# A three-stage attention and expert kernel: the conversion of one weight matrix is moved from each expert's first layer into its second

## The chip, the cores and the metric

The kernel runs on one core of a Trainium2 chip. The metric is the device time of one launch, in microseconds (us). The core has five engines that run their own instruction streams in order: TensorE (PE in the profile, with its weight loads as PEld), VectorE (DVE), ScalarE (ACT), GpSimd (POOL) and SyncE (SP, here only a queue that starts transfers). They wait for each other and for transfers through semaphores.

## The reference, cut to what matters

```python
def reference(**kwargs):
    attn_out = _attn_ref(**attn_kwargs)          # attention, the 32 largest scores of each row
    x = ...reshape(B * S, H * D)                 # 2304 rows of 512
    x = _moe_ref(x=x, **moe_kwargs)
    return _moe2_ref(x=x, **moe2_kwargs)

def _moe_ref(x, w_skip, w_gate, w1, w2):         # 8 experts, one per row, rows may skip
    ...
    for e in range(E):
        mask = e_idx == e
        h = np.maximum(xc[mask] @ w1[e], 0.0)    # 512 -> 1024, the expert's first layer
        y[mask] = gate_w[mask, None] * (h @ w2[e])  # 1024 -> 512, its second layer
    out[do_compute] = xc + y

def _moe2_ref(x, w_in, w_out):                   # every row
    h = x @ w_in                                 # 512 -> 2048, the up-projection
    g = h * (1.0 / (1.0 + np.exp(-1.702 * h)))
    return (g @ w_out).astype(np.float32)
```

`w_in` and `w_out` come as 64-bit floats; the other arrays are 32-bit.

## The kernel before, in words

The program has three stages, one after the other: attention with the choice of experts (up to about 507 us of the profiled span), the eight experts (to about 697 us), and the up- and down-projection over all 2304 rows (to the end).

**The experts.** They are done in eight turns of a Python loop, in an order that puts the four experts with most rows on the even turns. An even turn (from here on a long turn) has room for 192 rows, an odd one (a short turn) for 128. What each turn does on each engine follows from the order in which the loop writes the instructions; nothing reorders them.

- `layer1` runs 8 steps f, one for each 128 columns of `w1`. A step is 4 matmuls, which the trace shows as 8 records, so 64 in a turn; `ph` is a step's result in PSUM and has four buffers. In each step ACT writes the high part of the hidden values (`hb`, line 928), DVE the low part (line 930), and `step(f)` is called.
- `step(f)` calls `split_w2`: ACT makes the high part `w2h` of 128 rows of `w2` (line 967), DVE or POOL the low part `w2l` (line 968). At f = 0 POOL also gathers the rows `xg` of the next turn from DRAM, and at f = 0 and 4 it scatters finished rows `xo` to DRAM, where there are any.
- Between the layers PE transposes the gathered rows of the next turn (`turn`, lines 914 to 918: `xgT`).
- `layer2` multiplies `hb` with `w2h` and `w2l` (`py`, line 945): 40 matmuls in a long turn, of which 16 are for its second piece of 64 rows and come first, and 24 in a short one. ACT and DVE then combine the results (`yo`, lines 951 and 952, only in long turns; `xo`, lines 948 and 953).

**The conversion of w_in.** `w_in` is cut into 16 pieces of 128 x 512 numbers. `split_f64` is a Python generator with three parts. The first starts the transfer of a piece of 64-bit numbers into `raw`; the second makes 32-bit numbers `t` of it with three DVE instructions (lines 865 to 867); the third makes a high part `wih` on ACT (line 870) and a low part `wil` on POOL (line 871). A long turn converts three pieces, a short turn one. In the kernel before, the pieces of a turn are asked for at the turn's start and at f = 0 and 4, and their second and third parts are written into the steps f = 2 to 7 of that same turn's `layer1`. `raw` has two buffers. The results are used only in the third stage.

**Transfers.** SP starts the loads of `w1` (2 MB a turn, `w1t`, two buffers), of `w2` (eight loads of 256 KB, one buffer each, so the load for the next turn waits until this turn's conversion has read the buffer) and of `raw` (512 KB each), in the order in which the program writes them. POOL starts gathers and scatters.

Of the kernel before, what the change touches and what calls it, by code (L numbers as in the profile page):

```python
# [11 lines left out]
I32 = mybir.dt.int32  # L12
AF = mybir.ActivationFunctionType
ALU = mybir.AluOpType
# [15 lines left out]
def body(ctx: ExitStack, tc: tile.TileContext, q, k, v, w_skip, w_gate, w1, w2, w_in, w_out, out):  # L30
    nc = tc.nc
    V, A, G, T, SY = nc.vector, nc.scalar, nc.gpsimd, nc.tensor, nc.sync
    P = 128
    B, H, S, D = q.shape
    NT, DM = out.shape
    E, _, F = w1.shape
    DFF = w_in.shape[1]
# [53 lines left out]
    def load_w1(e):  # L91
        w1t = ew.tile([P, KC, F], F32, name="w1t")
        if isinstance(e, int):
            SY.dma_start(w1t, w1[e].rearrange("(c p) f -> p c f", p=P))
        else:
            SY.dma_start(w1t, w1[bass.ds(e, 1), :, :].rearrange("o (c p) f -> p (o c) f", p=P))
        return w1t
# [19 lines left out]
    def fetch_rows(xg, ix, src=XD):  # L117
        G.indirect_dma_start(
            out=xg, out_offset=None, in_=src, in_offset=bass.IndirectOffsetOnAxis(ap=ix, axis=0)
        )  # L120
# [6 lines left out]
    with ExitStack() as ph:  # L127
# [116 lines left out]
        def warm(k):  # L244
            for _ in range(k):
                T.matmul(Y, ones[:, :P], ones, start=True, stop=True)
# [445 lines left out]
        todo = []  # L692
# [16 lines left out]
        for n in range(NTL + 17):  # L709
# [5 lines left out]
            if n == NTL // 2:  # L715
                w1t = load_w1(0)
# [140 lines left out]
            first_rows()  # L857

    def split_f64(pool, src, hi, lo, queue=SY):
        raw = pool.tile([P, DFF // 4, 2], I32, name="raw")  # L860
        queue.dma_start(raw.rearrange("p n w -> p (n w)"), src.bitcast(I32))
        yield
        t = pool.tile([P, DFF // 4], I32, name="t")
        u = pool.tile([P, DFF // 4], I32, name="u")
        V.tensor_scalar(t, raw[:, :, 1], 3, 0x3FFFFFF8, op0=ALU.logical_shift_left, op1=ALU.bitwise_and)
        V.scalar_tensor_tensor(u, raw[:, :, 1], -0x40000000, t, op0=ALU.bitwise_and, op1=ALU.bitwise_or)
        V.scalar_tensor_tensor(t, raw[:, :, 0], 29, u, op0=ALU.logical_shift_right, op1=ALU.bitwise_or)
        yield
        wf = t.bitcast(F32)
        A.activation(hi, wf, AF.Copy)  # L870
        G.tensor_tensor(lo, wf, hi.bitcast(F32), op=ALU.subtract)
        yield

    fw = ctx.enter_context(tc.tile_pool(name="fw", bufs=1))
# [4 lines left out]
    def out_weights(pool, pf):  # L879
        f = len(woh)  # L880
        woh.append(pool.tile([P, DM], F32R, name=f"woh{f}"))
        wol.append(pool.tile([P, DM], F32R, name=f"wol{f}"))
        return split_f64(pf, w_out[f * P : (f + 1) * P, :], woh[f], wol[f])


    with ExitStack() as ph:
        ph.enter_context(tc.manual_schedule())
        wt = ph.enter_context(tc.tile_pool(name="wt", bufs=2))
# [11 lines left out]
        def gather(tiles):  # L900
            xgs = []
            for ix, rows in tiles:
                xg = ew.tile([P, DM + 1], F32, name="xg", bufs=4)
                fetch_rows(xg[:rows], ix)
                xgs.append(xg)
            return xgs

        def turn(tiles, xgs):
            xgT = mp.tile([P, KC, NS], F32, name="xgT")
            o = 0  # L910
            for (_, rows), xg in zip(tiles, xgs):
                pt = pT.tile([P, KC, P], F32, name="pt")
                for c in range(KC):
                    T.transpose(pt[:, c, :rows], xg[:rows, c * P : (c + 1) * P], ident[:rows, :rows])
                if o:
                    A.activation(xgT[:, :, o : o + rows], pt[:, :, :rows], AF.Copy)
                else:
                    V.tensor_copy(xgT[:, :, :rows], pt[:, :, :rows])
                o += rows
            return xgT  # L920

        def layer1(w1t, xgT, ns, step):
            hb = mp.tile([P, FC1, 2 * NS], F32R, name="hb", bufs=1)
            for f in range(FC1):
                ph_ = pH.tile([P, NS], F32, name="ph")
                for c in range(KC):
                    T.matmul(ph_[:, :ns], w1t[:, c, f * P : (f + 1) * P], xgT[:, c, :ns], start=(c == 0), stop=(c == KC - 1))  # L927
                A.activation(hb[:, f, :ns], ph_[:, :ns], AF.Relu)
                for a, b in ((0, 2 * P), (P, NS))[: 1 + (ns > P)]:
                    V.scalar_tensor_tensor(hb[:, f, b : b + min(P, ns - a)], ph_[:, a : min(a + P, ns)], 0.0,  # L930
                                           hb[:, f, a : min(a + P, ns)].bitcast(F32), op0=ALU.max, op1=ALU.subtract)
                step(f)
            return hb

        def layer2(hb, ws, tiles, xgs):
            for (ix, rows), xg in reversed(list(zip(tiles, xgs))):
                py = pY.tile([P, DM], F32, name="py")
                xo = mp.tile([P, DM], F32, name="xo")
                if rows < P:
                    parts = [(P, 0), (P, 1)]  # L940
                else:
                    parts = [(0, 0), (0, 1), (2 * P, 0)]
                for f in range(FC1):
                    for u, (o, b) in enumerate(parts):
                        T.matmul(py, hb[:, f, o : o + P], ws[b][f], start=(f == 0 and u == 0),  # L945
                                 stop=(f == FC1 - 1 and u == len(parts) - 1))
                if rows == P:
                    V.scalar_tensor_tensor(xo, py, xg[:, DM:], xg[:, :DM], op0=ALU.mult, op1=ALU.add)  # L948
                else:
                    yo = mp.tile([P, DM], F32, name="yo", bufs=1)  # L950
                    A.activation(yo[:rows], py[rows:, :], AF.Copy)
                    V.tensor_tensor(yo[:rows], py[:rows, :], yo[:rows], op=ALU.add)
                    V.scalar_tensor_tensor(xo[:rows], yo[:rows], xg[:rows, DM:], xg[:rows, :DM], op0=ALU.mult, op1=ALU.add)
                late.append((ix, xo[:rows]))

        def scatter():
            ix, xo = late.pop(0)
            G.indirect_dma_start(
                out=X2D, out_offset=bass.IndirectOffsetOnAxis(ap=ix, axis=0), in_=xo, in_offset=None,
            )  # L960
# [11 lines left out]
        todo = []  # L972
        for c in range(KC):
            for u in range(4):
                us = slice(u * DFF // 4, (u + 1) * DFF // 4)
                todo.append(split_f64(wt, w_in[c * P : (c + 1) * P, us], wih[:, c, us], wil[:, c, us],
                                      SY if todo[1:] else A))

        turns = [0, 4, 1, 5, 2, 6, 3, 7]
        slots = []  # L980
        for k in turns:
            slots.append([(IXS[:, k, :1], P)] + ([(IXS[: NS - P, k, 1:], NS - P)] if k < BIGS else []))
        who = [0]
        for k in turns[1:]:
            who.append(nc.values_load(flags[:, 2 + E + k : 3 + E + k], engines=[mybir.EngineType.SP], min_val=0, max_val=E - 1))
        nxt = []
        xgs = x0
        warm(10)
        nx = turn(slots[0], xgs)
        for e in range(E):  # L990
            w1n = load_w1(who[e + 1]) if e + 1 < E else None
            long = turns[e] < BIGS
            ns = NS if long else P
            convs = [todo.pop(0) for _ in range(1 if e % 2 else 3)]
            ws = ([], [])

            def step(f):
                split_w2(raws, ws, f, long)
                if f == 0:
                    for g in convs[:2]:  # L1000
                        next(g)
                    if e + 1 < E:
                        nxt.append(gather(slots[e + 1]))
                if f in (0, 4) and late:
                    scatter()
                for k, g in enumerate(convs):
                    if f - 2 * k in (2, 3):
                        next(g)
                if f == 4 and len(convs) > 2:
                    next(convs[2])  # L1010

            hs = layer1(w1t, nx, ns, step)
            if e + 1 < E:
                raws = load_w2(who[e + 1])
                nx = turn(slots[e + 1], nxt[-1])
            layer2(hs, ws, slots[e], xgs)
            if e + 1 < E:
                xgs = nxt[-1]
                w1t = w1n

        while late:
            scatter()
        todo = [out_weights(fw, wt) for _ in range(2)]
        for _ in range(3):
            for g in todo:
                next(g)
        A.activation(padf, padf, AF.Sigmoid)
        warm(31)
# [2 lines left out]
    with ExitStack() as ph:  # L1031
        ph.enter_context(tc.manual_schedule())
        fw = ph.enter_context(tc.tile_pool(name="fw2", bufs=1))
        wt = ph.enter_context(tc.tile_pool(name="wt2", bufs=2))
# [4 lines left out]
        todo = [None, None] + [out_weights(fw, wt) for _ in range(2, FC2)]  # L1039
# [69 lines left out]
        for b in range(len(blocks)):  # L1109
            po = [pO.tile([P, DM], F32, name=f"po{t}") for t in range(blocks[b][1] // P)]  # L1110
            for f in range(FC2):
                gs = up(b, x, f)
# [49 lines left out]
```

## Time and profile before

| | |
|---|---|
| three runs, median (lowest to highest) | 1116.03 us (1115.49 to 1120.85) |
| the profiled execution: its own time, and its span | 1116.85 us, 1115.0 us |
| busy share of the span: PE, PEld, DVE, ACT, POOL | 91%, 76%, 63%, 56%, 40% |
| the experts, first `layer1` matmul to the last `py` | 184.01 us, from 512.71 to 696.72 us |
| TensorE clock granted over the span, as a share of full speed | 0.971 |

The span runs from the first to the last instruction of the profiled execution; its own time is 1.85 us longer. Busy shares are means over three stages with different limits, so a change within the experts is read from rows of that stretch.

### The profile page before, as it was taken

What the parts mean: (1) busy time and instruction counts of PE and PEld (TensorE: products, weight loads), DVE (VectorE), ACT (ScalarE), POOL (GpSimd) and SP (SyncE); (2) the same over time, 40 slices, a digit from 0 to 9 for tenths busy, and PEclk for the clock granted to TensorE, in tenths of its full rate; (3) what the DMA queues carried; (4) which work ended last, traced back from release to release, by engine and by line L of the source; (5) the groups of instructions that cost most, each with busy time, mean ns of one, the idle gap of its engine ahead of it and who ended that gap; (6) DMA issues with size and microseconds to landing.
All of it is one profiled execution on the core that took longest, in us unless ns stands there. A gap on an engine that the chain in (4) does not pass through costs nothing. (4 is left out here: it accounts for less than half of the span.)

```text
span 1115.0 us, 20235 instructions
## 1 busy us (share of the span) xinstructions
PE 1017.0 (91%) x6523; PEld 848.8 (76%) x6523; DVE 706.9 (63%) x3376; ACT 622.1 (56%) x1426; POOL 449.0 (40%) x584
## 2 busy tenths in 40 slices
PE   6899999899999999877879778999999999999998
PEld 3777777787777777765768667688888878888887
DVE  7988889988998899944655666566322223222232
ACT  5999999999999999932233333333222222222232
POOL 4777777767777777713435354222000000000000
PEclk8999999999999999988889889999999999999999
DMA  4211141154111310036677673332100010010010
GB/s 102 48 33 33 32 119 29 36 187 122 37 37 37 83 54 16 2 86 212 225 258 275 231 245 134 136 120 95 59 18 1 19 58 1 1 57 1 0 39 19
DMA packets 98803, 91.86 MB, mean 82 GB/s; under 512 B 71680, under 2 KB 71680, under 8 KB 98688
## 3 DMA queue, kind: packets, MB, share of 16 engines
q1 hardware_dynamic: 96704, 84.17, 24.6%
q0 software_dynamic: 1696, 5.25, 1.4%
q8 instruction: 54, 0.88, 0.3%
q10 hardware_dynamic: 288, 1.05, 0.3%
q14 instruction: 61, 0.50, 0.2%
HBM read 72.38 MB, written 17.05 MB: 80 GB/s over the span
## 5 line engine op out<-in xcount | busy, mean ns | idle before, releaser
L275 DVE MAX8 C<-s 128x8 f32<-128x72 f32 x1152 | 217.9, 221 | 2.2 <-ACT s L268 2.2
L307 POOL TENSOR_TENSOR z<-s,z 128x576 f32<-128x576 f32 x144 | 203.2, 1411 | 4.3 <-ACT z L302 4.0
L1070 DVE TENSOR_TENSOR g<-phh,g 128x512 f32<-128x512 f32 (+1 forms) x80 | 51.1, 638 | 178.8 <-ACT g L1069 178.8
L1069 ACT ACTIVATE g<-phh 128x512 f32<-128x512 f32 (+1 forms) x80 | 44.3, 553 | 168.0 <-PE phh L1067 168.0
L409 PE MATMUL Y<-vn,AT 128*128 128x65 f32 x1024 | 121.4, 272 | 0.0
L409 PEld LDWEIGHTS Y<-vn,AT 128*128 128x128 f32 x1024 | 119.4, 192 | 0.0
L302 ACT ACTIVATE z<-s,T 128x576 f32<-128x576 f32 x144 | 116.4, 808 | 2.8 <-DVE T L291 2.8
L339 ACT ACTIVATE k<-s,BT 128x576 bf16<-128x576 f32 x144 | 115.3, 801 | 0.4
L1082 PE MATMUL po<-woh,gh 128*128 128x512 f32 x288 | 112.7, 391 | 1.9 <-DVE ot L1091 1.7
L353 PE MATMUL pt<-ident,a 128*128 128x128 f32 x576 | 113.1, 283 | 1.2 <-POOL z L307 1.0
L268 ACT ACTIVATE s<-SS 128x576 f32<-128x576 f32 x144 | 96.8, 673 | 30.7 <-PE SS L262 28.6
L1082 PE MATMUL po<-wol,gh 128*128 128x512 f32 x288 | 112.4, 390 | 0.0
L1082 PE MATMUL po<-woh,gl 128*128 128x512 f32 x288 | 112.3, 390 | 0.0
L334 POOL TENSOR_SCALAR a<-s,BT 128x576 f32<-128x576 f32 x144 | 107.3, 745 | 0.5 <-POOL BT L296 0.4
L312 DVE MAX8 z<-z 128x8 f32<-128x576 f32 x144 | 107.0, 743 | 0.0
L354 PE MATMUL pt<-nident,k 128*128 128x128 bf16 x576 | 105.1, 221 | 0.0
L927 PE MATMUL ph<-xgT,w1t 128*128 128x192 f32 (+1 forms) x512 | 76.9, 312 | 17.8 <-DVE hb L930 17.2
L260 PE MATMUL SS<-kT,qT 64*128 64x256 f32 x512 | 73.6, 407 | 19.6 <-ACT s L268 19.6
L353 PEld LDWEIGHTS pt<-ident,a 128*128 128x128 f32 x576 | 83.8, 146 | 9.4 <-POOL z L307 1.2
L342 ACT ACTIVATE AT<-pt 128x512 f32<-128x512 f32 x144 | 89.8, 623 | 0.2 <-PE pt L354 0.2
L927 PEld LDWEIGHTS ph<-xgT,w1t 128*128 128x128 f32 x512 | 74.2, 198 | 20.0 <-issue 17.6
L1074 DVE TENSOR_TENSOR gl<-g,gh 128x512 fp32r<-128x512 f32 (+1 forms) x80 | 51.2, 639 | 52.5 <-ACT gh L1072 47.1
(233 smaller groups left out, 2151.8 us busy)
## 6 DMA issues: line engine op xcount, KB each, us to landing
w1t<-in_moe_w_dram SPq DMA_DIRECT2D x8, 2048.0 KB, 8.5
w<-in_moe_w_dram SPq DMA_DIRECT2D x64, 256.0 KB, 3.4
raw<-in_moe_w_out_dram SPq DMA_DIRECT2D x16, 512.0 KB, 3.3
raw<-in_moe_w_in_dram SPq DMA_DIRECT2D x14, 512.0 KB, 8.9
xr<-X2D SPq DMA_DIRECT2D x18, 256.0 KB, 3.7
out_dram<-ot SPq DMA_DIRECT2D x18, 256.0 KB, 2.2
qn<-in_q_dram SPq DMA_DIRECT2D x32, 128.0 KB, 2.9
kn<-in_k_dram SPq DMA_DIRECT2D x32, 128.0 KB, 2.9
```

What stands on the lines that cost most here:

```text
L268: A.activation(s, SS[:, SLOT[j] : SLOT[j] + S], AF.Copy, scale=SC)
L275: V.max(C[:, g, :], s[:, g * SEG : (g + 1) * SEG])
L302: A.activation(z, d["s", c], AF.Sign, bias=T24[:, n, 7:8], scale=-1.0 - 2.0 ** -20, accum_out=sg)
L307: G.tensor_tensor(z, d["s", c], z, op=ALU.mult)
L312: V.max(z8, d.pop(("z", c)))
L334: G.tensor_scalar(a[:, o : o + S], d.pop(("s", c)), BT[:, n, :1], 1.0, op0=ALU.add, op1=ALU.mult)
L339: A.activation(d["k", r][:, o : o + S], d["s", c], AF.Relu, bias=BT[:, n, 1:], scale=-BIG)
L353: T.matmul(out, a, ident, is_transpose=True, start=True, stop=False)
L354: T.matmul(out, d["k", r][:, sl], nident, start=False, stop=True)
L409: T.matmul(y[:, w * j : w * j + w], t[:, 4 * j + g, :], d["v"][:, g, j, :], start=False, stop=(j == 1 and g == 3))
L927: T.matmul(ph_[:, :ns], w1t[:, c, f * P : (f + 1) * P], xgT[:, c, :ns], start=(c == 0), stop=(c == KC - 1))
L1082: T.matmul(po[t], lh[:, ts_], rh[f], start=(f == 0 and u == 0), stop=(f == FC2 - 1 and u == 2))
```

## The change

The second and third parts of all of a turn's pieces are taken out of `layer1` and written between `layer1` and `layer2`, one piece after the other. The transfers of the next turn's pieces are asked for right behind them, also ahead of `layer2`. `raw` gets a third buffer, and the scratch tile `u` goes: the three DVE instructions now work in `t` in place. The load of `w1` is written one turn further ahead, behind the loads of `w2`. Of the first turn's three pieces, the third is now started from ACT's queue like the first two. The first two pieces of `w_out` are asked for before the last `layer2` and converted after it.

```diff
     def split_f64(pool, src, hi, lo, queue=SY):
-        raw = pool.tile([P, DFF // 4, 2], I32, name="raw")
+        raw = pool.tile([P, DFF // 4, 2], I32, name="raw", bufs=3)
...
-        u = pool.tile([P, DFF // 4], I32, name="u")
         V.tensor_scalar(t, raw[:, :, 1], 3, 0x3FFFFFF8, op0=ALU.logical_shift_left, op1=ALU.bitwise_and)
-        V.scalar_tensor_tensor(u, raw[:, :, 1], -0x40000000, t, op0=ALU.bitwise_and, op1=ALU.bitwise_or)
-        V.scalar_tensor_tensor(t, raw[:, :, 0], 29, u, op0=ALU.logical_shift_right, op1=ALU.bitwise_or)
+        V.scalar_tensor_tensor(t, raw[:, :, 1], -0x40000000, t, op0=ALU.bitwise_and, op1=ALU.bitwise_or)
+        V.scalar_tensor_tensor(t, raw[:, :, 0], 29, t, op0=ALU.logical_shift_right, op1=ALU.bitwise_or)
...
-                                      SY if todo[1:] else A))
+                                      SY if c or u > 2 else A))
...
+        def take(e):
+            gs = [todo.pop(0) for _ in range(1 if e % 2 else 3)]
+            for g in gs:
+                next(g)
+            return gs
+
+        w1s = [w1t, load_w1(who[1])]
+        ahead = take(0)
         for e in range(E):
-            w1n = load_w1(who[e + 1]) if e + 1 < E else None
...
-            convs = [todo.pop(0) for _ in range(1 if e % 2 else 3)]
...
-                if f == 0:
-                    for g in convs[:2]:
-                        next(g)
...
-                for k, g in enumerate(convs):
-                    if f - 2 * k in (2, 3):
-                        next(g)
-                if f == 4 and len(convs) > 2:
-                    next(convs[2])
-
-            hs = layer1(w1t, nx, ns, step)
+
+            hs = layer1(w1s.pop(0), nx, ns, step)
+            convs = ahead
             if e + 1 < E:
                 raws = load_w2(who[e + 1])
                 nx = turn(slots[e + 1], nxt[-1])
+            if e + 2 < E:
+                w1s.append(load_w1(who[e + 2]))
+            for g in convs:
+                next(g)
+                next(g)
+            if e + 1 < E:
+                ahead = take(e + 1)
+            else:
+                first_out = [out_weights(fw, wt) for _ in range(2)]
+                for g in first_out:
+                    next(g)
             layer2(hs, ws, slots[e], xgs)
...
-        todo = [out_weights(fw, wt) for _ in range(2)]
-        for _ in range(3):
-            for g in todo:
+        for _ in range(2):
+            for g in first_out:
                 next(g)
```

How this moves instructions is shown at three places; line numbers of the changed kernel are one smaller there, and the numbers behind names tell buffers apart.

On DVE in the first layer of turn 2 (a long one), steps f = 1 to 4 stood so before:

```order
L968 TENSOR_TENSOR w2l_1_11841<-w2_1_11756,w2h_1_11840 128x512
L930 SCALAR_TENSOR_TENSOR hb_11812<-ph_11844,hb_11812 128x128
L930 SCALAR_TENSOR_TENSOR hb_11812<-ph_11844,hb_11812 128x64
L865 TENSOR_SCALAR t_11856<-raw_11825 128x512
L866 SCALAR_TENSOR_TENSOR u_11857<-raw_11825,t_11856 128x512
L867 SCALAR_TENSOR_TENSOR t_11856<-raw_11825,u_11857 128x512
L930 SCALAR_TENSOR_TENSOR hb_11812<-ph_11861,hb_11812 128x128
L930 SCALAR_TENSOR_TENSOR hb_11812<-ph_11861,hb_11812 128x64
L968 TENSOR_TENSOR w2l_3_11870<-w2_3_11760,w2h_3_11869 128x512
```

and stand so now:

```order
L967 TENSOR_TENSOR w2l_1_11839<-w2_1_11746,w2h_1_11838 128x512
L929 SCALAR_TENSOR_TENSOR hb_11814<-ph_11842,hb_11814 128x128
L929 SCALAR_TENSOR_TENSOR hb_11814<-ph_11842,hb_11814 128x64
L929 SCALAR_TENSOR_TENSOR hb_11814<-ph_11854,hb_11814 128x128
L929 SCALAR_TENSOR_TENSOR hb_11814<-ph_11854,hb_11814 128x64
L967 TENSOR_TENSOR w2l_3_11863<-w2_3_11750,w2h_3_11862 128x512
```

The three instructions that read `raw` are gone from between the `hb` instructions, on which PE's next matmuls wait.

On DVE in the second layer of the same turn, before:

```order
L968 TENSOR_TENSOR w2l_7_11934<-w2_7_11768,w2h_7_11933 128x512
L918 COPY xgT_11955<-pt_11956 128x4x128
L952 TENSOR_TENSOR yo_11980<-py_11962,yo_11980 64x512
L953 SCALAR_TENSOR_TENSOR xo_11963<-yo_11980,xg_11666 64x512
L948 SCALAR_TENSOR_TENSOR xo_11985<-py_11984,xg_11664 128x512
L930 SCALAR_TENSOR_TENSOR hb_12013<-ph_12014,hb_12013 128x128
```

and now:

```order
L917 COPY xgT_11930<-pt_11931 128x4x128
L864 TENSOR_SCALAR t_11939<-raw_11781 128x512
L865 SCALAR_TENSOR_TENSOR t_11939<-raw_11781,t_11939 128x512
L866 SCALAR_TENSOR_TENSOR t_11939<-raw_11781,t_11939 128x512
L864 TENSOR_SCALAR t_11945<-raw_11783 128x512
...
L866 SCALAR_TENSOR_TENSOR t_11951<-raw_11785,t_11951 128x512
L951 TENSOR_TENSOR yo_11977<-py_11959,yo_11977 64x512
L952 SCALAR_TENSOR_TENSOR xo_11960<-yo_11977,xg_11663 64x512
L947 SCALAR_TENSOR_TENSOR xo_11982<-py_11981,xg_11661 128x512
L929 SCALAR_TENSOR_TENSOR hb_12008<-ph_12009,hb_12008 128x128
```

All nine instructions of the turn's three pieces now stand between the copy of `xgT` and the results of `layer2`, ahead of the first `hb` of the next turn.

On ACT at the end of that turn, before:

```order
L928 ACTIVATE hb_11812<-ph_11925 128x192
L967 ACTIVATE w2h_7_11933<-w2_7_11768 128x512
L870 ACTIVATE wih_11332<-t_11920 128x512
L951 ACTIVATE yo_11980<-py_11962 64x512
L928 ACTIVATE hb_12013<-ph_12014 128x128
```

and now:

```order
L927 ACTIVATE hb_11814<-ph_11902 128x192
L966 ACTIVATE w2h_7_11910<-w2_7_11758 128x512
L869 ACTIVATE wih_11332<-t_11939 128x512
L869 ACTIVATE wih_11332<-t_11945 128x512
L869 ACTIVATE wih_11332<-t_11951 128x512
L950 ACTIVATE yo_11977<-py_11959 64x512
L927 ACTIVATE hb_12008<-ph_12009 128x128
```

Three high parts instead of one stand ahead of `yo`, and the first `hb` of the next turn stands behind it as before. On SP the loads of turns 1 to 7 keep their order (`w2` of a turn, `w1` of the turn after, the turn's pieces of `raw`); only the third piece of turn 0 leaves its place between the first `w1` and the first `w2` there.

## Rows read from the trace of the kernel before

**Rows 1.** Stretches of turns: length, busy PE PEld DVE ACT POOL, clock, DMA, GB/s
```profile
602.36:634.74 32.38, 24.16 (x109) 20.91 (x109) 16.42 (x34) 8.83 (x20) 10.32 (x8) 0.84 0.78 272
682.17:696.72 14.55, 13.17 (x89) 11.46 (x88) 11.56 (x16) 6.56 (x17) 8.84 (x7) 1.00 0.20 64
...
sum 184.01, PE 152.74 PEld 131.76 DVE 115.21 ACT 62.70 POOL 82.05; mean PE 19.09 PEld 16.47 DVE 14.40 ACT 7.84 POOL 10.26
```

**Rows 2.** What PE waited for, 505 to 712 us: total, times, longest
```profile
PE ph L927 <- DVE hb L930: 17.2, 5, 6.0
PE py L945 <- DVE hb L930: 7.4, 5, 1.7
PE pt L914 <- DMA xg<-XD,IXS: 3.8, 3, 1.9
```

**Rows 3.** PE in order of time, turns 4 and 5: start, duration
```profile
602.36 9.28 PE L927 MATMUL ph<-xgT,w1t 128*128 128x192 f32 x56
617.67 2.90 PE L927 MATMUL ph<-xgT,w1t 128*128 128x192 f32 x8 [6.03 <-DVE hb L930]
...
622.43 0.39 PE L945 MATMUL py<-w2h,hb 128*128 128x512 f32 x1
622.66 0.39 PE L945 MATMUL py<-w2l,hb 128*128 128x512 f32 x1
...
634.74 7.31 PE L927 MATMUL ph<-xgT,w1t 128*128 128x128 f32 x64
642.75 1.05 PE L914 MATMUL pt<-ident,xg 128*128 128x128 f32 x8 [0.70 <-DMA xg<-XD,IXS]
```

**Rows 4.** DVE in order of time, turn 4
```profile
615.31 0.43 DVE L865 TENSOR_SCALAR t<-raw 128x512 int32<-128x512 int32 x1 [8.05 <-DMA raw<-in_moe_w_in_dram]
...
616.50 0.69 DVE L867 SCALAR_TENSOR_TENSOR t<-raw,u 128x512 int32<-128x512 int32 x1
...
618.44 1.10 DVE L865 TENSOR_SCALAR t<-raw 128x512 int32<-128x512 int32 x1
619.58 1.64 DVE L866 SCALAR_TENSOR_TENSOR u<-raw,t 128x512 int32<-128x512 int32 x1
...
626.28 0.42 DVE L930 SCALAR_TENSOR_TENSOR hb<-ph,hb 128x128 fp32r<-128x128 f32 x2
...
627.21 0.69 DVE L918 COPY xgT<-pt 128x512 f32<-128x512 f32 x1
628.55 0.68 DVE L952 TENSOR_TENSOR yo<-py,yo 64x512 f32<-64x512 f32 x1 [0.65 <-ACT yo L951]
629.27 0.74 DVE L953 SCALAR_TENSOR_TENSOR xo<-yo,xg 64x512 f32<-64x512 f32 x1
634.94 0.75 DVE L948 SCALAR_TENSOR_TENSOR xo<-py,xg 128x512 f32<-128x512 f32 x1 [4.93 <-PE py L945]
```

**Rows 5.** POOL in order of time, turn 4
```profile
617.93 1.33 POOL L871 TENSOR_TENSOR wil<-t,wih 128x512 fp32r<-128x512 f32 x1 [7.72 <-ACT wih L870]
619.22 1.45 POOL L968 TENSOR_TENSOR w2l<-w,w2h 128x512 fp32r<-128x512 f32 x1
```

**Rows 6.** ACT in order of time, end of turn 4
```profile
626.40 0.63 ACT L870 ACTIVATE wih<-t 128x512 fp32r<-128x512 f32 x1 [2.31 <-DVE t L867]
627.92 0.59 ACT L951 ACTIVATE yo<-py 64x512 f32<-64x512 f32 x1 [0.89 <-PE py L945]
```

**Rows 7.** SP's queue in order of time, turn 4
```profile
602.64 14.90 SPq L861 DMA_DIRECT2D raw<-in_moe_w_in_dram  x3
```

**Rows 8.** Transfers by stretch (columns as in rows 1): a busy one, turns 4 and 5
```profile
630.00:635.00 5.00, 5.00 (x23) 4.09 (x22) 0.07 (x2) 0.00 (x0) 0.00 (x0) 0.89 1.01 403
602.36:650.04 47.68, 38.32 (x206) 33.20 (x205) 29.34 (x51) 15.66 (x38) 21.30 (x17) 0.89 0.73 249
```

**Rows 9.** Gathers, median us from start to landing: 590 to 597, 606 to 620 us
```profile
xg<-XD,IXS POOLq DMA_INDIRECT x2, 4.5
...
xg<-XD,IXS POOLq DMA_INDIRECT x1, 8.0
```

More of the change, by code (lines that the diff above doesn't have):

```diff
@@ L998, in step @@
                 split_w2(raws, ws, f, long)
-                if f == 0:
-                    for g in convs[:2]:
-                        next(g)
-                    if e + 1 < E:
-                        nxt.append(gather(slots[e + 1]))
+                if f == 0 and e + 1 < E:
+                    nxt.append(gather(slots[e + 1]))
                 if f in (0, 4) and late:
                     scatter()
-                for k, g in enumerate(convs):
-                    if f - 2 * k in (2, 3):
-                        next(g)
-                if f == 4 and len(convs) > 2:
-                    next(convs[2])
-            hs = layer1(w1t, nx, ns, step)
+            hs = layer1(w1s.pop(0), nx, ns, step)
+            convs = ahead
             if e + 1 < E:
@@ L1018, in body @@
                 xgs = nxt[-1]
-                w1t = w1n
         while late:
             scatter()
-        todo = [out_weights(fw, wt) for _ in range(2)]
-        for _ in range(3):
-            for g in todo:
+        for _ in range(2):
+            for g in first_out:
                 next(g)
```

## The prediction

> **What bounds the kernel now.** I read the busy times by stretch first, one stretch for each turn of the experts. The reader is to see that the eight turns take 184.0 us, that PE is busy in 152.7 of them, and that a long turn (32.4 us for turn 4) runs at a granted clock of 0.84, while the last turn runs at 1.00 [rows 1]. So a long turn loses time twice: PE waits, and part of its work is done at the lower of its two clock levels (1.2 instead of 2.4 GHz). The waits of PE name the first cause: 17.2 us before layer-1 matmuls, all for DVE's `hb`, and 7.4 us before layer-2 matmuls, for `hb` too [rows 2].
>
> PE and DVE in order of time show how this comes about in turn 4. PE runs 56 records in 9.28 us, then stands 6.03 us, and the last eight take 2.90 us instead of the 1.33 us that 8/56 of 9.28 gives [rows 3]. DVE stands 8.05 us until 615.31 us for a piece of `raw`, with `hb` queued behind it [rows 4]. SP had asked for that piece from 602.64 us on, right behind the 2 MB of `w1` [rows 7]. It is there 12.95 us after the turn's start (602.36), but its place in the program is at step f = 2, so DVE is ready for it at about 607. The conversions that follow run beside POOL's subtractions [rows 5] and keep `hb` late into layer 2. The wait is one of place: nothing in the turn uses what PE is held up for.
>
> **The change part by part.** I work out a long turn, a short turn and the last turn as they should stand, and set their sum against 184.0.
>
> *Layer 1 of a long turn.* Without the `raw` instructions PE needs 64 records at 9.28/56 = 0.166 us, 10.6 us. The four transposes take half of 1.05 us, 0.5. Layer 2 is 40 matmuls, 0.23 us apart (622.43 to 622.66), 9.1 [rows 3]. Together 20.2 us if nothing waits.
>
> *The moved work, counted from the end of layer 1 (0).* DVE still has the last `hb`, `w2l` and `xgT`, which run from 626.28 to 627.90 back to back [rows 4]; with ACT's part ahead of them I put their end at 2.5. A piece costs DVE 1.88 us where nothing is beside it (615.31 to 617.19 [rows 4]; the last of its three instructions starts at 616.50). Where two POOL subtractions fall into it, its first two instructions take 1.10 and 1.64 us, and with the third it ends 3.5 us after its start at 618.44 [rows 4, 5]. The first piece now has no POOL work beside it; the second and the third each meet one subtraction, that of the piece before. Three pieces cost between 3 x 1.88 = 5.6 and 1.88 + 2 x 3.5 = 8.9 us; I take 7.1, nearly the middle, since each meets one POOL instruction and not two. DVE is then at 9.6, just where PE ends layer 2 (0.5 + 9.1), so this cover is all used. Queued behind it are a high part on ACT (as long as `yo`, 0.59) and `yo` itself [rows 6], DVE's `yo` and two `xo` (0.68, 0.74, 0.75 [rows 4]), 3.4 us, and with hand-overs 13.1; then the next turn's first `hb`, at 13.3. PE starts the next layer 1 at 9.6 and has four `ph` buffers, four steps of 7.31/8 = 0.91 us [rows 3]: it asks for that `hb` at 13.3. The two meet. I put 0.5 us on each long turn for this: 20.7. The bounds are 0 and, with 8.9 for the pieces and one more POOL subtraction of 1.33 [rows 5] ahead of `xo`, 3.1 us.
>
> Here the Trainium skill, SBUF — State Buffer, section "Who interferes with whom", speaks against the new place: a DVE instruction with two SBUF inputs and a GpSimd instruction that reads SBUF shut each other out for the whole instruction. The trace agrees (1.10 and 1.64 us beside POOL, without POOL the first takes 0.43 and the third 0.69). By that rule the second and third piece would cost 1.88 + 1.33 each, the pieces 8.3 us, and the long turns together some 5 us more than in my sum.
>
> *The transfers.* SP's order from turn 1 on is the old one, so a long turn's pieces are asked for at its start as before, though now all three at once; before, the third waited for the first to be converted, and SP with it for 14.9 us [rows 7]. The first was there 12.95 us after the turn's start with two in flight; DVE now wants it at 10.6 + 2.5 = 13.1. One more 0.5 MB at the mean of a busy stretch (403 GB/s [rows 8]) is 1.3 us. I take 0 to 1 us of wait, within the 0.5 above. Earlier loads of `w1` and the third buffer then cost nothing: their cover is a whole turn. Should it go, the case below prices it.
>
> *A short turn.* 7.31 us of layer 1, 1.05 of transposes and 24 matmuls of 0.23 us, 5.5, make 13.9. PE waits there for gathered rows, 0.7 us in turn 5 [rows 3], at most 1.9 in any [rows 2]. The gather is issued from POOL at the same step as before, but transfers will be denser, so I take 1.9, and 0.4 for small waits: 16.2. The one piece (1.88 us) lies in the 5.5 us of layer 2, ahead of `xo`.
>
> *The last turn* has neither gather nor transposes: 7.31 + 5.5 and 0.3 for small waits, 13.1, against 14.55 before [rows 1]. The two pieces of `w_out`, converted behind it, lie as before beside the wait for the last scatter. In the third stage `raw` has three buffers instead of two and nothing else is moved; in `t` in place DVE does the same three instructions. Both at 0: DVE and SP have slack there, since PE sets that stage's pace throughout.
>
> *Sum.* 4 x 20.7 + 3 x 16.2 + 13.1 = 144.5, against 184.0: 39.5 us less. The profiled execution took 1116.85 us by itself, which gives 1077.3. The median of the runs is 0.8 lower; I forecast 1077 us.
>
> **The rivals.**
>
> *Nothing is left waiting.* 4 x 20.2 + 3 x 13.9 + 12.8 = 135.3, 48.7 us less: 1068. For it speaks that the last turn's clock is 1.00; against it, that the gather's wait is not touched.
>
> *DVE becomes the bound in the long turns.* The pieces take 8.9 us and POOL's subtractions delay `xo`, so each of four turns waits 3.1 us instead of 0.5, and the clock falls as it did after the 6.03 us, at 1.6 us (2.90 less 1.33 [rows 3]): 4 x 4.2 = 17, so 1094. For it: the cover is used to the last tenth. Against it: each piece meets one subtraction, not two.
>
> *The transfers become the bound.* Turns 4 and 5 moved 249 GB/s x 47.68 us = 11.9 MB at a busy share of 0.73 [rows 8]. The same bytes in 20.7 + 16.2 = 36.9 us need 322 GB/s, and at a full share 249/0.73 = 341 GB/s. Then backlog reaches into the short turns, where a gather that lands 4.5 us after its start beside light traffic needs 8.0 beside heavy [rows 9]: 3.5 us more wait and 1.6 of clock in three turns, 15 us: 1092. Against it: 403 GB/s in the densest 5 us [rows 8]. The Trainium skill, DMA: Bandwidth & Descriptors, section "Specifications", gives some 358 GB/s as a core's limit from HBM; by it the pair needs 33 of the 36.9 us. That stretch exceeded it, though only for 5 us.
>
> *The wait only moves.* DVE runs in order, so a piece that is late in layer 2 holds `xo` and the next `hb` one for one. It is level with before where the pieces are there some 10 us later than 13.1 after a turn's start (39.5/4), and slower by 0.5% from 11.5 us later: 1122 or more. Against it: 12.95 us was measured with the same loads ahead [rows 4, 7].
>
> *The change gains nothing*, because PE's stalls also cover something else that is due then, transfers above all: 1116. Against it: with a share of 0.73 [rows 8] they have room.
>
> **How the numbers follow.** The forecast (1070 to 1085) 0.55; nothing waits 0.07; DVE 0.14; transfers 0.17; no gain 0.03; slower 0.04. The range of 1068 to 1094 takes in the first four. A change of 0.5% (5.6 us) is about what these runs tell from none, as their three times lie 5.4 us apart: faster 0.93, same 0.03, slower 0.04.
>
> **What would show it.** PE's waits for `hb` before layer-1 matmuls fall from 17.2 to under 3 us; the clock in long turns rises from 0.84 to over 0.95; a long turn takes 20 to 22 us, a short one 15 to 17; DVE's three conversions stand in one block in layer 2, the second and third longer than 1.88 us. Wrong would be: a wait for `raw` in layer 2, waits for `xg` over 3 us, or for the first `hb` of a short turn over 2.

## The result, and the profile after

The changed kernel takes 1084.35 us (median of 4 runs, 1081.44 to 1085.91) against 1115.76 us (4 runs): a ratio of 0.9713, interval 0.9679 to 0.9747. Forecast were 1077 us and a range of 1068 to 1094.

The busy times by stretch of the changed kernel, one line for each turn of the experts (columns as in rows 1), answer to [rows 1]:

```profile
514.75:535.84 21.09, 20.34 (x109) 18.41 (x110) 14.63 (x31) 8.89 (x20) 8.34 (x7) 1.00 1.01 393
535.84:551.49 15.65, 13.85 (x98) 12.46 (x96) 12.65 (x19) 7.77 (x19) 10.79 (x10) 1.00 0.58 188
551.49:572.20 20.71, 20.14 (x109) 18.27 (x108) 17.31 (x32) 8.07 (x19) 10.04 (x8) 1.00 1.02 387
572.20:588.08 15.88, 14.04 (x98) 12.54 (x97) 12.46 (x19) 8.52 (x20) 11.40 (x10) 1.00 0.72 236
588.08:608.60 20.52, 20.15 (x110) 18.27 (x109) 17.17 (x32) 8.05 (x18) 10.24 (x8) 1.00 0.99 377
608.60:626.08 17.48, 15.75 (x97) 13.71 (x96) 12.57 (x20) 8.47 (x20) 12.78 (x10) 0.90 0.80 261
626.08:646.56 20.48, 20.13 (x109) 18.27 (x108) 17.13 (x32) 8.06 (x18) 9.02 (x7) 1.00 0.95 351
646.56:659.83 13.27, 13.15 (x90) 11.47 (x88) 11.88 (x18) 7.41 (x18) 9.26 (x7) 1.00 0.24 74
sum 145.08, PE 137.56 PEld 123.42 DVE 115.80 ACT 65.25 POOL 81.88; mean PE 17.19 PEld 15.43 DVE 14.48 ACT 8.16 POOL 10.23
```

The reader is to see three things. The eight turns take 145.1 us instead of 184.0. PE is busy in 137.6 of them instead of 152.7, although it runs the same matmuls: the granted clock in long turns is 1.00, where turn 4 had 0.84. And in the long turns the DMA engines are now full (0.95 to 1.02), while DVE's busy time over the eight turns is what it was (115.8 against 115.2).

The waits of PE in the experts and the hand-over, as in [rows 2]:

```profile
PE pt L913 <- DMA xg<-XD,IXS: 7.3, 7, 1.8
...
PE po L1107 <- DMA xr<-X2D: 3.7, 2, 2.4
```

No wait for `hb` is left in the list; 17.2 and 7.4 us of it have gone. The waits for gathered rows grew from 3.8 us in three to 7.3 in seven, and the waits for `xr` (the rows that the third stage reads) in the hand-over to it grew to 3.7 us. In the kernel before they were:

```profile
PE po L1100 <- DMA xr<-X2D: 1.3, 3, 0.6
```

DVE in order of time in turn 4, as in [rows 4]:

```profile
601.32 0.41 DVE L864 TENSOR_SCALAR t<-raw 128x512 int32<-128x512 int32 x1
...
603.10 0.42 DVE L864 TENSOR_SCALAR t<-raw 128x512 int32<-128x512 int32 x1
603.56 0.69 DVE L865 SCALAR_TENSOR_TENSOR t<-raw,t 128x512 int32<-128x512 int32 x1
604.28 1.67 DVE L866 SCALAR_TENSOR_TENSOR t<-raw,t 128x512 int32<-128x512 int32 x1
...
607.05 1.66 DVE L866 SCALAR_TENSOR_TENSOR t<-raw,t 128x512 int32<-128x512 int32 x1
610.02 0.68 DVE L951 TENSOR_TENSOR yo<-py,yo 64x512 f32<-64x512 f32 x1 [1.31 <-ACT yo L950]
```

and POOL beside the second piece:

```profile
603.93 1.47 POOL L870 TENSOR_TENSOR wil<-t,wih 128x512 fp32r<-128x512 f32 x1 [6.81 <-ACT wih L869]
```

The three pieces stand in one block of 7.39 us (601.32 to 608.71), with no wait for `raw` ahead of any; in the second and the third the last instruction takes a microsecond longer than the 0.69 us it takes alone, beside a subtraction on POOL. `yo` then waits 1.31 us for ACT. SP's queue shows the other side, as in [rows 7]:

```profile
587.15 3.20 SPq L861 DMA_DIRECT2D raw<-in_moe_w_in_dram  x3
591.86 10.97 SPq L106 DMA_DIRECT2D w<-in_moe_w_dram  x8
```

The three requests take 3.20 us instead of 14.90, and the loads of `w2` begin 1.5 us after the last of them.

**Where the time went, span by span.** The profiled executions differ by 1116.85 - 1084.05 = 32.8 us. The experts gave 38.9. The hand-over, from the last layer-2 matmul to the first matmul of the third stage, grew by 2.8 us (659.83 to 673.65 against 696.72 to 707.78), and the third stage by 1.4 (673.65 to 1082.3 against 707.78 to 1115.0). The attention stage, which the change does not touch, ended 2.0 us later (514.75 against 512.71).

### The profile page after: what moved, and what is told of

The parts are those of the page before. It is cut to its first block, busy times and chain, and to the rows that moved or that the text cites. A ratio compares the mean times of both kernels' runs of the same rounds, so it can differ in the third digit from the quotient of the medians.

```text
span 1082.3 us, 20240 instructions
## 1 busy us (share of the span) xinstructions
PE 1005.8 (93%) x6523; PEld 843.2 (78%) x6523; DVE 709.9 (66%) x3376; ACT 625.2 (58%) x1426; POOL 450.4 (42%) x584
## 4 chain that ended last, share of the span: by engine, by line
PE 42%; DMA 4%; issue 2%; DVE 2%; POOL 1%; ACT 1%; SPq 0%; POOLq 0%; ACTq 0%; DVEq 0%
PE phh L1074 18%; PE po L1089 18%; DMA xg<-XD,IXS 4%; PE py L944 3%; PE ph L926 2%; POOL w2l L967 1%; DVE w2l L967 1%; DMA out_dram<-ot 1%; PE pt L1063 1%; PE pt L913 1%; PE pt L897 0%; POOL wil L870 0%; POOL X2D L957 0%; DVE t L865 0%; DVE ot L1098 0%
## 5 line engine op out<-in xcount | busy, mean ns | idle before, releaser
L339 ACT ACTIVATE k<-s,BT 128x576 bf16<-128x576 f32 x144 | 115.2, 800 | 0.4
L1074 PE MATMUL phh<-xh,wih 128*128 128x512 f32 (+1 forms) x320 | 81.3, 376 | 0.2 <-ACT xh L1112 0.2
L1079 ACT ACTIVATE gh<-g 128x512 fp32r<-128x512 f32 (+1 forms) x80 | 47.2, 590 | 56.4 <-DVE g L1077 56.4
```

Source lines behind the costliest of these rows:

```text
L339: A.activation(d["k", r][:, o : o + S], d["s", c], AF.Relu, bias=BT[:, n, 1:], scale=-BIG)
L1074: T.matmul(phh[:, :n], lh[:, c, fs], rh[:, c, :n], start=(u == 0 and c == 0), stop=(u == 2 and c == KC - 1))
```

## The experiments

Each was timed against the kernel before on the same chip (1117.13 us for the first four, 1118.26 for the last four; 1115.76 beside the changed kernel). So times of kernels that were timed in different rounds can differ by some 2.5 us for that alone, and ratios to the kernel before compare them better. "Experts" is the time from the first `layer1` matmul to the last `py`, "hand-over" that from there to the first matmul of the third stage.

**1. The place alone.** The kernel before, with this edit:

```diff
-                for k, g in enumerate(convs):
-                    if f - 2 * k in (2, 3):
-                        next(g)
...
                 nx = turn(slots[e + 1], nxt[-1])
+            for g in convs:
+                next(g)
+                next(g)
             layer2(hs, ws, slots[e], xgs)
```

> The kernel before with one edit: the second and third parts of a turn's pieces stand between the layers; all transfers are asked for where they were, with two raw buffers. Theory of place (the gain comes from taking the wait for raw out of layer 1): the waits for hb before layer-1 matmuls go. The third piece must now wait for its buffer until the first is converted, 15.0 us after the turn's start, and lands 3 to 5 us later, when DVE wants it at 17.5; SP's loads of w2 stand behind it. So 1 to 4 us of each long turn come back: the experts take 149 to 162 us instead of 184.0 (145.1 in the changed kernel), and the time is 1086 to 1100 us. Theory of loads (the third buffer and the earlier requests bring it): the experts still take over 172 us, and the time is over 1104 us.

Measured: 1100.16 us (ratio 0.9846, interval 0.9812 to 0.988), experts 160.5 us. That is within the span of the theory of place for the experts (149 to 162), at its slow end, and a hair over its span for the time (1086 to 1100). Of the stalls before layer-1 matmuls 3.3 us are left, but PE now waits for gathered rows:

```profile
PE pt L914 <- DMA xg<-XD,IXS: 14.8, 7, 4.7
...
PE ph L927 <- DVE hb L930: 3.3, 4, 1.6
```

SP's queue in that kernel says why: the third piece waits for its buffer, and 17.07 us pass over the three requests.

```profile
598.86 17.07 SPq L861 DMA_DIRECT2D raw<-in_moe_w_in_dram  x3
616.18 4.36 SPq L106 DMA_DIRECT2D w<-in_moe_w_dram  x8
```

The eight loads of `w2`, the 2 MB of `w1` and the next piece are then asked for in one go, from 5.4 us ahead of the short turn to its start (621.53), and run beside its gather. Over turn 3 of that kernel the DMA engines are busy at 0.92, against 0.72 in turn 3 of the changed kernel, and the gathers of turns 3 and 5 land 6.4 and 7.2 us after their start (medians of two), against 4.7 and 4.4. I had put the loss into the long turns (a late third piece: 5.7 us of DVE waits for `raw` in four). But turn 4 takes 21.1 us there, little more than the changed kernel's 20.5, and turns 3 and 5 take 21.0 and 20.6 instead of 15.9 and 17.5: the loss came in the short ones.

**2. The loads alone.** The changed kernel, with the conversions back in `layer1`:

```diff
+                for k, g in enumerate(convs):
+                    if f - 2 * k in (2, 3):
+                        next(g)
...
-            hs = layer1(w1s.pop(0), nx, ns, step)
-            convs = ahead
+            convs = ahead
+            hs = layer1(w1s.pop(0), nx, ns, step)
...
-            for g in convs:
-                next(g)
-                next(g)
             if e + 1 < E:
                 ahead = take(e + 1)
```

> The changed kernel with the conversions put back into steps f = 2 to 7 of layer 1; the third raw buffer, the earlier requests and the order of the loads stay. Theory of place: the first piece still lands some 11 to 13 us after a long turn's start and is wanted at 4 to 5, so PE stalls as before; the experts take 176 to 186 us and the time is 1108 to 1119 us. Theory of loads: the experts take under 160 us and the time is under 1095 us.

Measured: 1117.93 us (1.0013, 0.9989 to 1.0037), experts 180.9 us. PE's waits are those of before:

```profile
PE ph L926 <- DVE hb L929: 16.8, 6, 7.2
PE py L944 <- DVE hb L929: 6.6, 4, 1.7
```

The theory of loads falls: the third buffer, the earlier requests and the order of the loads by themselves give nothing that can be measured.

**3. The last turn's piece behind the last scatters.**

```diff
-            for g in convs:
+            for g in convs if e + 1 < E else []:
...
         while late:
             scatter()
         for _ in range(2):
-            for g in first_out:
+            for g in convs + first_out:
```

> The changed kernel with the last turn's one piece converted behind the last scatters, with the two pieces of w_out. Theory of the hand-over queue (the last xo waits on DVE and the last scatter on POOL behind that piece): from the end of the last layer-2 matmul to the first matmul of the third stage it takes 11 to 12 us instead of 13.8, the experts as before 145, and the time is 1.5 to 4 us less, 1080 to 1083 us. Rival (the hand-over is longer for the loads of xr or the clock alone): it stays at 13 to 14.5 us and the time at 1084.

Measured: 1081.64 us (0.9666, 0.9628 to 0.9704), hand-over 11.74 us instead of 13.82, as the theory of the hand-over queue has it. The experts, expected at 145 us, take 148.3 in this profile, with 9.2 us of waits for `xg`, though the edit doesn't touch them before their last turn. The single times overlap with those of the changed kernel (1076.11 to 1084.0 against 1081.44 to 1085.91), so what the edit is worth is read from the hand-over in the trace and not from the time. POOL in the changed kernel:

```profile
661.34 1.37 POOL L870 TENSOR_TENSOR wil<-t,wih 128x512 fp32r<-128x512 f32 x1 [4.08 <-ACT wih L869]
662.88 1.24 POOL L957 DMA_INDIRECT X2D<-xo,IXS  x1 [0.16 <-issue]
```

and in this one:

```profile
663.51 0.97 POOL L957 DMA_INDIRECT X2D<-xo,IXS  x1 [3.79 <-DVE xo L947]
665.77 1.44 POOL L870 TENSOR_TENSOR wil<-t,wih 128x512 fp32r<-128x512 f32 x1 [1.28 <-ACT wih L869]
```

The last scatter starts 1.0 us after the last layer-2 matmul (662.52) instead of 3.05 (659.83), since the subtraction no longer stands ahead of it and DVE goes straight to `xo`. The other profiles divide the same way. Where the last turn's piece stands ahead of the last scatter, the hand-over takes 12.75 to 13.82 us (the changed kernel and experiments 1, 4, 5, 7 and 8); where it does not, 11.0 to 11.74 (the kernel before and experiments 2, 3 and 6).

**4. Two `raw` buffers in the third stage.**

```diff
-        raw = pool.tile([P, DFF // 4, 2], I32, name="raw", bufs=3)
+        raw = pool.tile([P, DFF // 4, 2], I32, name="raw", bufs=n)
...
-        todo = [None, None] + [out_weights(fw, wt) for _ in range(2, FC2)]
+        todo = [None, None] + [out_weights(fw, wt, 2) for _ in range(2, FC2)]
```

> The changed kernel with two raw buffers in the third stage, as before, and three in the experts. Rival on the hand-over (the third load of w_out, started right behind the loads of xr, delays their second half): the wait of 1.30 us before the second eight transposes falls under 0.5 and the hand-over is 1 to 2.5 us shorter. Theory of the hand-over queue: the hand-over stays within 0.7 us of 13.8, and the time at 1084.

Measured: 1082.52 us (0.9684, 0.965 to 0.9719), hand-over 13.72 us; the wait before the second eight transposes is 1.09 us. The third buffer there is not the cause; pricing it at 0 was right.

**5. The gather first.**

```diff
+                if f == 0 and e + 1 < E:
+                    nxt.append(gather(slots[e + 1]))
                 split_w2(raws, ws, f, long)
-                if f == 0 and e + 1 < E:
-                    nxt.append(gather(slots[e + 1]))
```

> The changed kernel with the next turn's gather written ahead of the first w2l at f = 0 instead of behind it. Theory (the waits for xg, 7.3 us in all, 1.7 to 1.8 us in each of turns 1, 3 and 5, come from POOL's place of the gather, not from full transfers): each gather starts 1.3 to 2.3 us earlier and lands as much earlier; the waits fall to under 2.5 us in all, the experts take 138 to 142 us instead of 145.1, and the time is 3 to 7 us under that of the changed kernel, 1077 to 1081. Rival (transfers set the landing): the waits stay over 5.5 us and the time within 2 us of 1084.

Measured: 1078.69 us (0.9671, 0.9641 to 0.9701), experts 140.3 us, as forecast. What was left of the wait:

```profile
PE pt L913 <- DMA xg<-XD,IXS: 1.9, 3, 0.8
```

In the changed kernel these waits come from POOL's order: the gathers take no less time here (5.9 us from start to landing in the median of ten, 5.2 in the changed kernel), but started earlier, beside the same loads, most of them are in time.

**6. Both of these.** The edits of experiments 3 and 5 on the changed kernel.

> The gather first and the last turn's piece behind the last scatters, both on the changed kernel. If both causes are apart from each other, the two gains add: experts 138 to 142 us, hand-over 11 to 12 us, time 1075 to 1079 us. Rival (one takes back the other): not faster than the better of the two alone.

Measured: 1077.12 us (5 runs; 0.9636, 0.9622 to 0.9651), experts 142.0 us, hand-over 11.34 us. This is the fastest kernel of the study by its median, 7.2 us under the changed one, where the two alone are 5.7 (experiment 5) and 2.7 us (experiment 3) under it; by their ratios the steps are 0.8%, 0.4% and 0.5%. Over experiment 5 alone it gains 1.6 us, less than the spread of single runs, and the intervals of the two ratios overlap. So the hand-over shows both gains together, and the times don't show that they add.

**7. The third piece of long turns twice on DVE.**

```diff
+        if twice:
+            V.tensor_scalar(t, raw[:, :, 1], 3, 0x3FFFFFF8, op0=ALU.logical_shift_left, op1=ALU.bitwise_and)
+            V.scalar_tensor_tensor(t, raw[:, :, 1], -0x40000000, t, op0=ALU.bitwise_and, op1=ALU.bitwise_or)
+            V.scalar_tensor_tensor(t, raw[:, :, 0], 29, t, op0=ALU.logical_shift_right, op1=ALU.bitwise_or)
         yield
...
-                                      SY if c or u > 2 else A))
+                                      SY if c or u > 2 else A, u == 2))
```

> The changed kernel with the three DVE instructions of each long turn's third piece done twice, 1.9 us more of DVE in layer 2 of four turns; the result is the same. Theory (the chain on DVE and the next turn's PE meet with less than 0.7 us to spare): the wait for the first hb of turns 1, 3, 5 and 7 appears, 1.2 to 2.5 us in each, some with a lower clock, so the experts take 150 to 160 us and the time is 5 to 14 us over that of the changed kernel, 1089 to 1098. Rival (DVE has several us of slack there): the experts stay within 2 us of 145.

Measured: 1094.27 us (0.9779, 0.9763 to 0.9796), experts 152.9 us. The wait for the first `hb` is there, four times, at most 2.0 us:

```profile
PE ph L930 <- DVE hb L933: 5.6, 4, 2.0
```

Of 4 x 1.9 = 7.6 us of added work PE waits for 5.6, so a long turn had in the mean about 0.5 us to spare; the single waits of 0.96 to 2.00 us put it between nothing and 0.9. The experts lose 7.9 us in all: beside the 5.6, the waits for `xg` grew by 0.7 (to 8.0 us), and after the wait of 2.00 us the next 32 records take 5.46 us instead of 3.84, at a granted clock of 0.68.

**8. Place and third buffer.** Experiment 1 with three `raw` buffers and the conversion in place in `t`; the requests stand where the kernel before has them.

> The first experiment with three raw buffers instead of two (and the conversion in place in t, for the room); the transfers are still asked for where the kernel before asks for them. Theory (with the place changed, the third buffer is what the rest hangs on, since SP is no longer held up until the third piece has its buffer; the turn in which the program writes the requests does not matter): the experts take 144 to 149 us instead of 160.5, the waits for xg fall from 14.8 to under 10 us, and the time is 1081 to 1087 us. Rival (it is the earlier requests): the experts stay over 155 us and the time over 1094.

Measured: 1084.98 us (0.9712, 0.9693 to 0.9732), experts 147.5 us, waits for `xg` 7.9 us. This is the changed kernel's ratio (0.9713). The turn in which the program writes the requests, and the earlier load of `w1`, are worth nothing that can be measured. The third buffer, with the conversion in place that makes room for it, is worth 1100.16 - 1084.98 = 15.2 us, but only together with the place: experiment 2 has it without the place and gains nothing.

## Why the prediction held, point by point

**What bounded the kernel** was named rightly: PE stood for the place of the wait for `raw`, and lost clock by it. Experiments 1, 2 and 8 show it from both sides: place alone 0.9846, loads alone 1.0013, place and third buffer 0.9712. So nothing is gained without the place, and the place alone brings about half of the gain.

**Turn by turn.** Long turns were put at 20.7 us and take 20.5 to 21.1, in the mean 20.7. Short turns were put at 16.2 and take 15.65, 15.88 and 17.48, the last of them over the 15 to 17 that was named as a sign. The last turn, put at 13.1, takes 13.27. The sum was 144.5, and 145.1 is measured. Inside the long turns the 0.5 us is another's, though: it was put there for `hb`, and no wait for `hb` is listed, but the gather is now late there too (0.35 to 0.74 us), since layer 1 no longer stands still for it. That this number came out is luck. The three pieces were put at 7.1 us, near the middle of two bounds, and take 7.39. The Trainium skill (SBUF — State Buffer, "Who interferes with whom") calls the sharing between DVE and GpSimd an exclusive lock, and by that the prediction had 8.3, each piece longer by POOL's whole subtraction. The trace shows less: a meeting cost 0.97 to 0.98 us, while the subtraction beside it took 1.47. In turn 4 it starts (603.93) beside an instruction that isn't longer for it (0.69 us), and 0.35 us ahead of the one that is.

**The transfers** were there in time: in turn 4 the pieces land 12.7 us after their request (median of three), the first request comes 0.9 us ahead of the turn, and DVE takes the first piece 13.2 us after the turn's start. What the third buffer's loss would cost, "the case below", was priced there at 15 us in the short turns' gathers, and that is where experiment 1 lost it and about what it measured (15.2 us between experiments 1 and 8); it was the expectation of experiment 1 that looked for it in the long turns. So the rival of full transfers is real, a third buffer away.

**DVE as the bound** was a fair rival: in the mean about 0.5 us is left in a long turn (experiment 7).

**The step that failed** is the one on the last turn. It adds up PE's work (7.31 + 5.5 + 0.3) and puts what comes behind it at 0, for the two pieces of `w_out` "lie as before beside the wait for the last scatter". They do: on POOL they stand behind that scatter in both kernels. But the turn's own piece of `w_in` stands in no sum. It was converted in layer 1 before. Now it stands ahead of the last `xo` on DVE and ahead of the last scatter on POOL, and SP's loads of `xr`, with which the third stage begins, wait for that scatter. In the kernel before the scatter starts 1.23 us after the last layer-2 matmul (696.72), in the changed kernel 3.05:

```profile
697.95 0.97 POOL L958 DMA_INDIRECT X2D<-xo,IXS  x1 [2.55 <-DVE xo L948]
```

The hand-over is 2.8 us longer, of which the scatter's later start is 1.8. Experiment 3 takes back 2.1 of them, experiment 4 none. The other 1.4 us are the third stage's first matmuls at the lower clock. In the changed kernel they are

```profile
673.65 2.08 PE L1074 MATMUL phh<-xh,wih 128*128 128x512 f32 x4 [0.17 <-ACT xh L1112]
675.52 1.91 PE L1074 MATMUL phh<-xh,wil 128*128 128x512 f32 x4
```

and in the kernel before

```profile
707.78 1.48 PE L1067 MATMUL phh<-xh,wih 128*128 128x512 f32 x4 [0.48 <-ACT xh L1105]
709.10 1.09 PE L1067 MATMUL phh<-xh,wil 128*128 128x512 f32 x4
```

These are not shown to come from the piece: experiment 3, without it, still has 2.07 and 1.55 us there, and experiments 5 and 8, with it, have 1.48 and 1.08, 1.49 and 1.09. What lowers the clock there stays open.

**The remaining 2.0 us** lie in the attention stage, whose code is the same. Its end varies from execution to execution: 512.71 us in the profile of before, which the forecast was summed against, and 513.9 to 519.4 in the profiles of the eight experiments. It goes with the granted clock of the first 50 us: in the four profiles where that is 0.90 (the kernel before and experiments 2, 3 and 5) the stage ends at 512.7 to 514.2 us, in the six where it is 0.86 or 0.80 (the changed kernel among them, at 0.86) at 514.8 to 519.4. What sets that clock was not tried and stays open, as does why a wait of 1.66 us in turn 5 cost clock (0.90) and waits of 1.80 and 1.84 us in turns 1 and 3 did not (1.00).

## What to carry to other kernels

Work that nothing near it needs belongs behind the last result that the next matmuls wait for, in a stretch where its engine has time to spare; ask on which engines its every part queues, also POOL's, and what the end of the loop has behind it. An in-order queue of loads with one buffer too few holds up all the loads behind it, and the price shows where these then meet other transfers. A prefetch alone is worth nothing where the consumer stands too early.

## What the runs showed of the hardware that I had not expected

With loads of 256 KB to 2 MB queued one behind the other, one core moved 393, 387 and 377 GB/s over three of the four long turns (20.5 to 21.1 us, DMA share 0.99 to 1.02; the fourth 351 at 0.95), more than the some 358 GB/s that the Trainium skill (DMA: Bandwidth & Descriptors, "Specifications") gives as its limit from HBM. DVE's first conversion instruction, which reads `raw` alone, takes 0.41 us by itself and up to 2.22 us beside POOL work (turn 1), so it isn't only the instructions with two inputs that get longer there; the prediction listed the 1.10 us of this instruction under a rule for two inputs.
